# Linear attention and channel mix on one core: the order of work from a table, and q of five batches transposed by the DMA crossbar

## The chip, the core and the metric

The kernel runs on one core of a Trainium2 chip. The core has TensorE (PE, matmuls; its weight loads are shown as PEld), VectorE (DVE), ScalarE (ACT), GpSimd (POOL) and SyncE (SP). Matmuls write to PSUM, which has eight banks per partition; DVE and ACT carry results from PSUM to SBUF. DMAs are issued from the queues of POOL, SP and ACT. Each engine runs its instructions in program order and waits on semaphores.

The metric is the device time of one execution in microseconds, the median of several runs. Times inside the text come from one profiled execution.

## The reference

There are B = 8 batches, H = 8 heads, S = 576 positions, head size 64, so C = 512; the mix has an inner width of 1024.

```python
kv = np.einsum('bhsd,bhse->bhde', k, v)
out = np.einsum('bhsd,bhde->bhse', q, kv)
rms = np.sqrt(np.mean(out * out, axis=-1, keepdims=True) + 1e-06)
x = out / rms * g_norm                       # then heads side by side: (B, S, 512)
x_prev = x moved by one position, zero in front
xk = mu_k * x + (1.0 - mu_k) * x_prev
xr = mu_r * x + (1.0 - mu_r) * x_prev
k = np.maximum(xk @ w_k, 0.0)
v = k * k @ w_v
r = 1.0 / (1.0 + np.exp(-(xr @ w_r)))
return r * v
```

Inputs and output are float32; the kernel computes with bf16 operands, cast on the way in by the loads.

## The kernel before

**Stages.** The work is cut into named pieces, and the names below are those of the table in the change. A number after the name is the batch (attention) or the group (mix), the part after the dot a head pair or a chunk, and `#2` a second piece of the same name.

Attention, per batch, over four head pairs `hp`; everything is held with channels on partitions and positions along the row:
- `loadk`, `loadv`, `loadq` (L314): from DRAM, 96 positions rows by heads, cast to bf16, on POOL's queue. Batch 0 comes in pieces of two heads, batch 1 in halves, the others whole. In batch 0 the first two heads come instead by `first_load` (L264), uncast, on SP's and ACT's queues, and are cast on DVE (L302).
- `kv` (L545): k times v for a head pair, on PE; `kvc`: its two diagonal blocks to SBUF.
- `qtr` (L572): q transposed on PE, 24 transposes of a 96x64 block for two head pairs; `qc` (L580): PSUM to the tile qT.
- `u` (L594): kv times qT on PE; `uc`: to the tile uT. `sq`: its square on DVE. `ss` (L620): sum over the channels of a head by a matmul with ones. `ln`, `exp` (L624, L628): the inverse root on ACT. `mul` (L641): x, into the tile xT, with a short copy that makes the shifted column block. `d`: x minus x_prev. `xk`, `xr` (L667): d scaled by a column (tile md) plus x_prev, into rings `xk`, `xr` of four batches.

Batch 0 has functions of its own (L381 on) that cut it finer, so that the mix can start early.

Mix, per group g of 512 positions, nine groups: `k` (eight chunks, L715), `relu` on ACT, `ksq` on DVE; `r` (four chunks, L766) and `sig` on ACT; `v` (four chunks in two parts); `out` on DVE, the product; `store` on SP (L696). `k`, `r` and `v` pieces are four matmuls of 128x512 each. Group 0's `k` is done in two halves, `k0.a` per head pair and `k0.b`. Group 1 needs the xk of batches 0 and 1.

**Weights.** `w_k0`, `w_k1`, `w_r`, `w_v` come on POOL's queue (L337); the first three are scaled by g_norm on DVE (`g.w_k0` and so on, L342).

**Buffers.** k, v, q, qT, uT and xT have two buffers, out has three. PSUM has two rings of two tiles of two banks: `mm` for the mix, `at` for the attention, batch 0 too.

**Order.** Every piece is added to a planner (L39) with the engines it may run on, the pieces it waits for, the buffers it uses, a duration and a due time. `run` (L78) places the pieces one by one by its own estimates, takes the due times of the STAGES list for the attention and T0 + TG * g for the mix, and then writes the instructions out in that order; each engine's order is fixed by it. While PE has a gap before the last of `k0.a`, `filler` (L684) puts matmuls of a zero tile there, their number from the gap's estimated length. In POOL's order the loads of batch 0 come first, then w_k0, w_k1, w_r, w_v, then batch 1 and the others.

Of the kernel before, what the change touches and what calls it, by code (L numbers as in the profile page):

```python
# [7 lines left out]
FP32 = mybir.dt.float32  # L8
# [4 lines left out]

class Buf:
    def __init__(self, tag):
        self.tag, self.users, self.t, self.placed = tag, [], None, False


class Piece:
    def __init__(self, on, fn, deps, bufs, due, rel, land, mode, table, name):  # L20
        self.on, self.fn, self.due, self.rel, self.land = on, fn, due, rel, land
        self.mode, self.table, self.name = mode, table, name
        self.deps = [d for d in deps if d is not None]
        self.bufs = list(bufs)
        for b in self.bufs:
            b.users.append(self)
        self.eng = self.start = self.end = None
        self.emitted = False


class Planner:
    TAIL = {"PE": 0.17, "ACT": 0.09, "DVE": 0.08, "POOL": 0.1, "SP": 0.0}
    LAT = {"PE": 0.06, "ACT": 0.06, "DVE": 0.06, "POOL": 0.1, "SP": 0.0}
    TO_PE = 0.1
    SWITCH = 0.1
    TABLE = 1.3
    COLD = 8.0
    WAIT = {"PE": 0.04, "ACT": 0.04, "DVE": 0.04, "POOL": 0.04, "SP": 0.04}

    def __init__(self, rings):  # L40
        self.rings = {tag: [None] * n for tag, n in rings.items()}
        self.left = []

    def add(self, on, fn, deps=(), bufs=(), due=0.0, rel=0.0, land=0.0, mode=None, table=None, name=""):
        p = Piece(on, fn, deps, bufs, due, rel, land, mode, table, name)
        self.left.append(p)
        return p

    def backward(self):
        after = {}  # L50
        for p in self.left:
            for d in p.deps:
                after.setdefault(d, []).append(p)

        def due(p):
            if p.due is None:
                us = min(p.on.values()) + max(self.TAIL[e] + self.LAT[e] for e in p.on) + 0.05
                p.due = min((due(s) for s in after.get(p, ())), default=1e6) - us
            return p.due

        for p in self.left:
            due(p)

    def room(self, bufs):
        t, want = 0.0, {}
        for b in bufs:
            if not b.placed:
                want.setdefault(b.tag, set()).add(b)
        for tag, bs in want.items():
            for old in self.rings[tag][:len(bs)]:  # L70
                if old is None:
                    continue
                if any(u.end is None for u in old.users):
                    return None
                t = max([t] + [u.end + 0.1 for u in old.users])
        return t

    def run(self, slack, filler=None, warm=None):  # L78
        self.backward()
        free, order, dma, hw = {}, [], 0.0, 0.0  # L80
        mode, table = "full", "ln"
        while self.left:
            best = {}
            for p in self.left:
                if any(d.end is None for d in p.deps):
                    continue
                room = self.room(p.bufs)
                if room is None:
                    continue
                ways = []  # L90
                for eng, us in p.on.items():
                    t = max(free.get(eng, 0.7), room, p.rel)
                    for d in p.deps:
                        if d.eng == eng and not d.land:
                            t = max(t, d.start + d.us + (0.05 if eng in ("ACT", "DVE") else 0.0))
                            continue
                        lat = self.LAT[d.eng]
                        if eng == "PE":
                            lat += self.TO_PE + slack(p)
                        t = max(t, d.end + lat)  # L100
                    late = 0.0
                    if eng == "PE" and p.mode != mode:
                        us = us + self.SWITCH
                    if eng == "PE" and t < self.COLD:
                        us = us * 1.9
                    if eng == "ACT" and p.table and p.table != table:
                        us, late = us + self.TABLE, 2.5 if p.table == "ln" else 0.0
                    ways.append((t + us, t, eng, us, late))
                _, t, eng, us, late = min(ways)
                best.setdefault(eng, []).append((t, p.due + late, p, us))  # L110
            picks = []
            for eng, c in best.items():
                t0 = min(x[0] for x in c)
                win = self.WAIT[eng]
                picks.append(min((x for x in c if x[0] <= t0 + win), key=lambda x: x[1] + x[0] * 0.1) + (eng,))
            t, _, p, us, p.eng = min(picks, key=lambda x: x[0])
            if p.eng == "PE":
                if filler and warm.end is None:
                    gap = t - free.get("PE", 0.7)
                    fill = filler(gap, free.get("PE", 0.7) > self.COLD)  # L120
                    if fill is not None:
                        n, fn = fill
                        f = Piece({"PE": 0.0}, fn, (), (), 0, 0, 0, "full", None, "idle%d" % n)
                        f.eng, f.start, f.end, f.us = "PE", free.get("PE", 0.7), t, gap
                        order.append(f)
                mode = p.mode
            if p.eng == "ACT" and p.table:
                table = p.table
            p.start, p.us = t, us
            free[p.eng] = t + us  # L130
            p.end = t + us + self.TAIL[p.eng]
            if p.land:
                if p.eng == "POOL":
                    dma = max(dma, t + us + 2.4) + p.land
                    p.end = dma + 1.3
                else:
                    hw = max(hw, t + us + 1.4) + p.land
                    dma = max(dma, hw)
                    p.end = hw + 1.3
            for b in p.bufs:  # L140
                if not b.placed:
                    b.placed = True
                    self.rings[b.tag].append(b)
                    self.rings[b.tag].pop(0)
            self.left.remove(p)
            order.append(p)
        for p in order:
            p.fn(p.eng)
            p.emitted = True
        return order  # L150
# [3 lines left out]
def kernel(  # L154
# [76 lines left out]
    def act_us(n, sbuf=False, ap=False):  # L231
        return 0.1 + n / 1200 + (0.03 if sbuf else 0.0) + (0.09 if ap else 0.0)
# [638 lines left out]
```

## Time and profile before

| | us |
|---|---|
| median of 5 runs (lowest, highest) | 224.34 (223.82, 225.93) |
| the profiled execution, its own time | 223.96 |
| its span, first to last instruction | 222.2 |
| PE busy | 205.1 |
| DVE busy | 154.1 |
| ACT busy | 134.8 |
| POOL busy | 27.3 |

In the span, PE's share is 92%; since matmuls are pipelined and their ends are modelled, idle time says more than that share. The granted clock of PE is 1.0 but for a stretch between 10 and 20 us. The page's slices show the DMA engines busy without a break up to about 72 us and little used afterwards, while PE has its gaps in the first third.

```profile
PE   8698779987998999999999999999999999999991
PEclk9959999999999999999999999999999999999999
DMA  6999999999999379537963300330033024016033
```

Each of 40 slices is 5.6 us; a digit is the busy share in tenths.

### The profile page before, as it was taken

The page shows a single profiled execution, that of the slowest core. Times are in us where ns is not written, and L with a number is a line of the kernel's source. Part 1 is how long each engine was busy: PE and PEld are TensorE (multiplying, and loading weights), DVE is VectorE, ACT ScalarE, POOL GpSimd, SP SyncE. Part 2 cuts the span into 40 slices and gives each one's busy share as a digit, 9 for nine tenths or more (in the row PEclk, how much of TensorE's full clock was granted, in tenths as well). Part 3 has the DMA queues.
Part 4 walks back from the last instruction along what each step waited for, and adds up shares of the span by engine and source line. Part 5 has one row for each costly group of instructions (what it writes and reads, how often), then busy time and mean ns, then how long its engine had stood idle before and what let it go on. Part 6 is the DMA issues. An engine that isn't in the chain of part 4 may idle for free.

```text
span 222.2 us, 4343 instructions
## 1 busy us (share of the span) xinstructions
PE 205.1 (92%) x1756; PEld 113.1 (51%) x1779; DVE 154.1 (69%) x311; ACT 134.8 (61%) x180; POOL 27.3 (12%) x42
## 2 busy tenths in 40 slices
PE   8698779987998999999999999999999999999991
PEld 8456555554554544454445864554444444444450
DVE  3459995699769999799928992999299424224231
ACT  2269364977489957964796479657965705504600
POOL 7862114042100021002100000000000000000000
PEclk9959999999999999999999999999999999999999
DMA  6999999999999379537963300330033024016033
GB/s 171 198 206 206 204 202 205 203 244 225 223 203 178 98 115 216 85 96 93 222 101 97 94 3 0 94 97 1 3 94 96 0 69 123 0 25 165 3 94 94
DMA packets 27592, 26.95 MB, mean 121 GB/s; under 512 B 1836, under 2 KB 23092, under 8 KB 27572
## 3 DMA queue, kind: packets, MB, share of 16 engines
q0 software_dynamic: 21008, 16.34, 47.8%
q1 hardware_dynamic: 5892, 9.45, 15.5%
q10 hardware_dynamic: 672, 0.89, 1.2%
q8 instruction: 14, 0.23, 0.4%
q14 instruction: 6, 0.05, 0.1%
HBM read 33.56 MB, written 9.44 MB: 194 GB/s over the span
## 4 chain that ended last, share of the span: by engine, by line
PE 50%; DMA 21%; DVE 15%; issue 4%; ACT 3%; POOL 3%; SPq 2%; POOLq 0%; DVEq 0%
PE mm L721 16%; PE mm L790 16%; PE mm L769 11%; DMA k<-in_k_dram 8%; DMA q<-in_q_dram 7%; DVE out L794 3%; DMA out_dram<-out 3%; DMA v<-in_v_dram 3%; DVE qT L222 3%; DVE md L669 2%; DVE sqk L728 2%; PE at L807 2%; PE at L596 2%; SPq L704 2%; PE mm L807 2%
## 5 line engine op out<-in xcount | busy, mean ns | idle before, releaser
L725 ACT ACTIVATE relu<-mm 128x1024 bf16<-128x1024 f32 x36 | 36.8, 1023 | 45.9 <-PE mm L721 39.1
L721 PE MATMUL mm<-xk,w_k 128*128 128x512 bf16 (+1 forms) x278 | 59.1, 355 | 1.2 <-issue 0.9
L790 PE MATMUL mm<-w_v,sqk 128*128 128x512 bf16 x248 | 57.6, 379 | 1.3 <-ACT sig L774 0.8
L794 DVE TENSOR_TENSOR out<-mm,sig 128x1024 f32<-128x1024 f32 x16 | 19.6, 1223 | 30.8 <-ACT ln L626 12.9
L790 PEld LDWEIGHTS <-sqk 128*128 128x128 bf16 x256 | 24.9, 98 | 28.2 <-issue 1.3
L721 PEld LDWEIGHTS <-w_k 128*128 128x128 bf16 x288 | 27.0, 98 | 24.1 <-issue 0.3
L769 PE MATMUL mm<-w_r,xr 128*128 128x512 bf16 x140 | 32.9, 380 | 1.6 <-DVE xr L492 1.3
L728 DVE TENSOR_TENSOR sqk<-relu 128x1024 bf16<-128x1024 bf16 x32 | 22.0, 687 | 9.9 <-ACT relu L725 9.8
L774 ACT ACTIVATE sig<-mm 128x1024 bf16<-128x1024 f32 x18 | 18.2, 1023 | 7.5 <-PE mm L769 7.3
L769 PEld LDWEIGHTS <-xr 128*128 128x128 bf16 x144 | 14.0, 98 | 16.9 <-DVE xr L492 1.9
L626 ACT ACTIVATE ln<-at,eps 128x576 f32<-128x576 f32 x28 | 19.3, 741 | 0.6 <-PE at L622 0.3
L229 ACT ACT_TABLE_LOAD x14 | 18.0, 1283 | 1.4 <-PEq L855 1.2
L669 DVE TENSOR_SCALAR md<-d,cols 128x576 bf16<-128x576 bf16 x56 | 18.5, 372 | 0.2
L630 ACT ACTIVATE rs<-ln 128x576 bf16<-128x576 f32 x28 | 17.8, 689 | 0.1
L220 ACT CAST uT<-at 128x576 bf16<-128x576 f32 (+1 forms) x25 | 15.0, 605 | 2.8 <-PE at L596 2.1
L316 POOL DMA_DIRECT2D k<-in_k_dram x11 | 8.0, 729 | 54.3 <-PE at L549 51.1
L220 ACT CAST kvb<-at 64x256 bf16<-64x256 f32 (+2 forms) x14 | 4.4, 316 | 14.3 <-PE at L549 7.8
L596 PE MATMUL at<-qT,kvb 128*128 128x288 bf16 x56 | 11.3, 286 | 1.8 <-ACT qT L220 0.9
L222 DVE COPY qT<-at 128x1152 bf16<-128x1152 bf16 (+2 forms) x17 | 11.1, 655 | 1.9 <-PE at L414 1.2
L692 PE MATMUL mm<-zero 128*128 128x128 bf16 x89 | 10.9, 285 | 1.1 <-DVE zero L271 1.1
L644 DVE TENSOR_TENSOR xT<-uT,rs 128x1152 bf16<-128x1152 bf16 x14 | 10.5, 750 | 1.1 <-ACT rs L630 1.1
L610 DVE TENSOR_TENSOR sq<-uT 128x1152 bf16<-128x1152 bf16 (+1 forms) x16 | 10.7, 678 | 0.6 <-ACT uT L220 0.3
(68 smaller groups left out, 200.3 us busy)
## 6 DMA issues: line engine op xcount, KB each, us to landing
out_dram<-out SPq DMA_DIRECT2D x22, 192.0 KB, 2.5
k<-in_k_dram POOLq DMA_DIRECT2D x6, 576.0 KB, 10.7
v<-in_v_dram POOLq DMA_DIRECT2D x6, 576.0 KB, 13.7
q<-in_q_dram POOLq DMA_DIRECT2D x6, 576.0 KB, 13.9
out_dram<-out SPq DMA_DIRECT2D x23, 128.0 KB, 2.4
out_dram<-out SPq DMA_DIRECT2D x22, 64.0 KB, 2.2
w_k<-in_moe_w_k_dram POOLq DMA_DIRECT2D x2, 512.0 KB, 8.5
w_v<-in_moe_w_v_dram POOLq DMA_DIRECT2D x1, 1024.0 KB, 15.6
```

The costliest lines, as they stand in the source:

```text
L220: nc.scalar.copy(out=dst, in_=src)
L229: nc.scalar.preload_act_table_set(name)
L626: nc.scalar.activation(out=get(ln), in_=ps.t[:, :, 0:HS], func=AF.Ln, bias=eps, scale=1.0 / HD)
L630: nc.scalar.activation(out=get(rs)[:, hp].rearrange("q (i c) -> q i c", i=2), in_=ln.t, func=AF.Exp, scale=-0.5)
L669: nc.vector.tensor_scalar(out=get(md)[:, hp], in0=d.t[:, hp], scalar1=cols[:, m0 + hp:m0 + hp + 1], scalar2=None, op0=ALU.mult)
L721: nc.tensor.matmul(get(ps)[:, fc % 2, a0:a1], w_k_sb[:, cc, 128 * fc:128 * fc + 128], xk[:, cc, x0:x0 + a1 - a0], start=(cc == 0), stop=(c ...
L725: nc.scalar.activation(out=get(rt), in_=ps.t, func=AF.Relu)
L728: nc.vector.tensor_mul(out=get(sqk)[:, 2 * f2:2 * f2 + 2, :], in0=rt.t, in1=rt.t)
L769: nc.tensor.matmul(get(ps)[:, ci % 2, :], xr[:, cc, n0:n0 + 128], w_r_sb[:, cc, :], start=(cc == 0), stop=(cc == NHP - 1))
L774: nc.scalar.activation(out=get(sg), in_=ps.t, func=AF.Sigmoid)
L790: nc.tensor.matmul(get(ps)[:, ci % 2, :], sqk.t[:, fc, 128 * ci:128 * ci + 128], w_v_sb[:, fc, :], start=(fc == 0), stop=(fc == NFC - 1))
L794: nc.vector.tensor_mul(out=get(ot)[:, xs, :], in0=ps.t[:, xs, :], in1=sg.t[:, xs, :])
```

## The change

1. The planner's search is gone. The order of all pieces, with the engine of those that have a choice and the number of idle matmuls in each gap, is a table in the file; `run` writes the pieces out in that order.
2. For batches 3 to 7 (`BY_DMA`) the pieces `qtr` and `qc` are replaced: `ql` copies q of a head pair into a tile `q2` (one buffer) with the two heads of the pair side by side, on DVE or ACT, and `qt` is one DMA per batch on SP's queue that transposes q2 into qT.
3. Batch 0 uses a PSUM ring of four single-bank tiles (`a1`). When the first tile of a later batch is asked for, that pool is released and the two-bank ring `at` is made in its place.
4. In batch 0 the scaling of d by a column is a piece of its own per head pair (`mk`, `mr`), on DVE or ACT, and `k0.a` may add up its head pairs in any order.
5. The first loads of v and q in batch 0 go with the others on POOL; k's stays on SP and is cast by ACT.
6. The shifted column block of `mul` is made by a second product instead of a copy.
7. From batch 4 on, the pieces that write the xk and xr rings also wait for the k and r pieces that read what they overwrite.

The table, cut after the last q transfer:

```diff
+ORDER = """
+loadq0.4 loadv0.6 loadk0.6 loadq0.6 setup loadv0.4 ident idle:42 kv0.3 qtr0.2 table loadk0.4 loadk0.2 qtr0.3
+qc0.3:DVE qc0.2#2:ACT idle:5 kv0.2 qc0.2:DVE kvc0.3#2:ACT small qc0.3#2:ACT kvc0.3:DVE idle:2 u0.3 kvc0.2#2:ACT
+kvc0.2:ACT idle:4 u0.2 first_k uc0.3:DVE sq0.3 u0.2#2 uc0.2#2:ACT loadq0.2 loadq0.0 idle:14 qtr0.0 cast_k:ACT qtr0.1
+uc0.2:DVE qc0.0#2:DVE ident9 qc0.1#2:ACT loadv0.2 qc0.0:DVE kv0.1 kvc0.1:ACT kvc0.1#2:ACT ss0.3 ln0.3 exp0.3
+qc0.1:DVE idle:7 u0.1 sq0.2 idle:1 ss0.2 uc0.1:DVE loadv0.0 sq0.1 ln0.2 tr9 cols exp0.2 kv0.0 kvc0.0:ACT idle:8
+ss0.1 sq0.2#2 kvc0.0#2:DVE idle:8 u0.0#2 ln0.1 u0.0 exp0.1 edge mul0.2 uc0.0#2:ACT uc0.0:DVE sq0.0 mul0.3 sq0.0#2
+loadv1.4 d0.2 mr0.2:DVE loadk1.4 ss0.2#2 ln0.2#2 exp0.2#2 idle:18 ss0.0 mul0.2#2 d0.2#2 ln0.0 exp0.0 loadv1.0 idle:7
+ss0.0#2 ln0.0#2 exp0.0#2 idle:25 kv1.2 kvc1.2:ACT mul0.1 d0.3 loadq1.0 qtr1.0 mul0.0 mk0.3:DVE d0.1 mul0.0#2
+mk0.1:DVE d0.0#2 kvc1.2#2:ACT d0.0 loadk1.0 idle:5 kv1.0 qc1.0:ACT loadq1.4 mr0.1#2:DVE kvc1.0#2:ACT mr0.3#2:ACT
+mr0.2#2:DVE idle:19 qtr1.2 kvc1.0:DVE u1.0 w_k1 xk0.3 qc1.2:DVE idle:13 u1.3 mr0.0:ACT uc1.0:ACT mk0.0:ACT uc1.3:ACT
+mk0.2:DVE xk0.2 u1.1 xk0.1 xk0.0 g.w_k1 mk0.2#2:DVE mk0.1#2:DVE xr0.0 mk0.0#2:ACT uc1.1:ACT w_k0 sq1.0 sq1.1 xk0.0#2
+idle:22 k0.a1.2 g.w_k0 mr0.3:ACT u1.2 mr0.0#2:ACT k0.a1.0 k0.a1.3 mk0.3#2:DVE xr0.2#2 ss1.0 uc1.2:ACT ln1.0 k0.a1.1
+w_r xk0.2#2 ss1.1 relu0.01 k0.a0.0 exp1.0 sq1.2 g.w_r:DVE k0.a0.3 k0.a0.1 sq1.3 xr0.2 k0.a0.2 relu0.00 ksq0.00
+ksq0.01 mr0.1:ACT k0.b1 xr0.1 k0.b0 ln1.1 w_v xr0.0#2 relu0.11 xr0.3 ksq0.11 ss1.2 relu0.10 ksq0.10 loadq2.0 exp1.1
+mul1.0 ss1.3 ln1.2 loadk2.0 r0.0 r0.1 sig0.0 v0.0.0 v0.0.1 v0.1.0 v0.1.1 out0.0 d1.0 xk1.0 exp1.2 ln1.3 exp1.3
+mul1.2 qtr2.2 d1.2 qc2.2:ACT r0.2 r0.3 sig0.1 xk1.2 v0.2.0 v0.2.1 v0.3.0 loadv2.0 kv2.0 kvc2.0#2:DVE loadq3.0
+kvc2.0:ACT ql3.2:ACT qtr2.0 ql3.3:DVE ql3.1:ACT v0.3.1 out0.1 ql3.0:DVE xr1.0 qc2.0:DVE k1.0 loadv3.0 k1.1 relu1.0
+u2.2 uc2.2:DVE qt3 k1.2 k1.3 relu1.1 ksq1.0 k1.4 k1.5 u2.3 uc2.3:ACT u2.0 uc2.0:DVE loadk3.0 k1.6 xr1.2 u2.1
+uc2.1:DVE loadq4.0 ql4.0:DVE relu1.2 k1.7 kv3.0 ksq1.2 relu1.3 r1.0 kvc3.0#2:ACT r1.1 sq2.0 ql4.1:DVE kvc3.0:ACT
+u3.1 ql4.2:DVE u3.0 r1.2 r1.3 store0.1 ql4.3:DVE ksq1.1 uc3.1:ACT uc3.0:ACT sig1.0 u3.3 ss2.0 ksq1.3 loadv5.0
+store0.0 v1.0.0 sig1.1 v1.0.1 loadv4.0 uc3.3:DVE ln2.0 ss2.1 ln2.1 sq2.2 exp2.0 v1.1.0 v1.1.1 out1.0 exp2.1 mul2.0
+loadk4.0 u3.2 store0.0#2 uc3.2:ACT ss2.2 loadk5.0 v1.2.0 ln2.2 exp2.2 ss2.3 sq3.0 sq3.2 v1.2.1 ln2.3 exp2.3 d2.0
+kv4.0 kvc4.0:ACT loadq5.0 kvc4.0#2:ACT kv5.0 store0.1#2 mul2.2 kvc5.0:ACT xk2.0 ss3.2 kvc5.0#2:ACT ln3.2 exp3.2 d2.2
+v1.3.0 ss3.3 ln3.3 xk2.2 ss3.0 ln3.0 exp3.3 qt4 v1.3.1 out1.1 xr2.0 ss3.1 u4.0 ln3.1 exp3.1 k2.0 k2.1 uc4.0:ACT
+xr2.2 relu2.0 exp3.0 u4.1 uc4.1:ACT k2.2 ksq2.0 k2.3 relu2.1 sq4.0 mul3.2 k2.4 d3.2 u4.3 uc4.3:ACT mul3.0 d3.0 u4.2
+uc4.2:ACT xk3.2 k2.5 loadv6.0 k2.6 k2.7 store1.0#2 relu2.2 ksq2.2 xk3.0 r2.0 r2.1 ksq2.1 relu2.3 ksq2.3 ql5.2:ACT
+xr3.2 ss4.1 loadk6.0 loadq6.0 r2.2 r2.3 sig2.0 sig2.1 ln4.1 exp4.1 ss4.0 k3.0 k3.1 ln4.0 relu3.0 store1.0 loadk7.0
+v2.0.0 ql5.1:DVE v2.0.1 v2.1.0 v2.1.1 ql5.0:DVE sq4.2 ss4.2 ln4.2 ss4.3 exp4.0 ql5.3:DVE v2.2.0 v2.2.1 qt5 out2.0
+ln4.3 v2.3.0 xr3.0 v2.3.1 ql6.3:ACT ksq3.0 exp4.3 exp4.2 out2.1 mul4.2 d4.2 ql6.0:DVE k3.2 k3.3 u5.2 uc5.2:DVE
+ql6.1:ACT relu3.1 ksq3.1 k3.4 k3.5 u5.0 relu3.2 ksq3.2 mul4.0 k3.6 k3.7 uc5.0:ACT relu3.3 u5.3 ksq3.3 u5.1 r3.0 r3.1
+uc5.1:DVE store1.1#2 uc5.3:ACT sq5.2 sq5.0 sig3.0 store2.0 store2.0#2 d4.0 xk4.0 kv6.0 kvc6.0#2:DVE r3.2 r3.3
+ql6.2:ACT ss5.1 sig3.1 kvc6.0:ACT store1.1 v3.0.0 v3.0.1 v3.1.0 ss5.3 store2.1 ln5.3 ln5.1 v3.2.0 store2.1#2 v3.1.1
+v3.2.1 loadv7.0 v3.3.0 xk4.2 out3.0 ss5.0 xr4.2 v3.3.1 out3.1 qt6 exp5.3 exp5.1 ss5.2 ln5.2 ln5.0 k4.0 k4.1 relu4.0
+k4.2 k4.3 relu4.1 u6.2 ksq4.0 xr4.0 u6.3 store3.0#2 loadq7.0 uc6.3:DVE exp5.0 exp5.2 uc6.2:DVE sq6.2 k4.4 k4.5
+relu4.2 k4.6 k4.7 mul5.0 u6.0 uc6.0:DVE ksq4.1 ksq4.2 relu4.3 mul5.2 ss6.3 ln6.3 ksq4.3 r4.0 r4.1 u6.1 sig4.0 kv7.0
+uc6.1:ACT r4.2 d5.2 xk5.2 d5.0 kvc7.0#2:ACT kvc7.0:DVE r4.3 xk5.0 sig4.1 sq6.0 v4.0.0 v4.0.1 ql7.2:ACT v4.1.0
+store3.0 v4.1.1 ql7.3:ACT store3.1 ql7.0:ACT v4.2.0 v4.2.1 ss6.2 v4.3.0 ql7.1:DVE v4.3.1 out4.0 store4.0 ln6.2 k5.0
+exp6.2 store3.1#2 out4.1 exp6.3 xr5.2 k5.1 relu5.0 ss6.1 k5.2 k5.3 ksq5.0 ln6.1 xr5.0 mul6.2 d6.2 k5.4 k5.5 relu5.1
+k5.6 exp6.1 k5.7 ss6.0 ksq5.1 xr6.2 relu5.2 relu5.3 ksq5.3 ln6.0 ksq5.2 r5.0 r5.1 qt7 u7.2 uc7.2:DVE store4.1 u7.3
 ...
```

The parts that make it work:

```diff
-    def run(self, slack, filler=None, warm=None):
...
+    def run(self, filler):
+        for token in ORDER:
+            name, _, eng = token.partition(":")
+            if name == "idle":
+                filler(int(eng))
+                continue
+            p = self.pieces[name]
+            assert not p.emitted and all(d.emitted for d in p.deps), name
+            p.fn(eng or p.on[0])
             p.emitted = True
...
+        "a1": (4, (128, 512), FP32),
+        "q2": (1, (NP, NHP, NJ, 2 * HD), BF16),
...
+            if buf.tag == "at" and len(at_pool) == 1:
+                at_pool[0].release()
+                at_pool[0] = pool = tc.alloc_tile_pool(name="psum_at", bufs=2, space=bass.MemoryType.PSUM,
+                                                       reuse_waits="tile")
...
+        if b in BY_DMA:
+            q2 = Buf("q2")
+            parts = []
+            for hp in range(NHP):
+                def q_relay(eng, hp=hp):
+                    copy(eng, get(q2)[:, hp].rearrange("p j (e d) -> p e j d", e=2),
+                         qin.t[:, 2 * hp:2 * hp + 2, :].rearrange("p e (j d) -> p e j d", j=NJ))
...
+            def q_turn(_):
+                nc.sync.dma_start_transpose(out=get(qT).rearrange("q i (j p) -> q (i j) p", j=NJ),
+                                            in_=q2.t.rearrange("p i j c -> p (i j c)"))
...
-        for hp0, n in groups[2]:
+        for hp0, n in groups[2] if b not in BY_DMA else ():
...
-                nc.vector.tensor_copy(out=xT.t[:, hs, 1:NP], in_=xT.t[:, hs, S:S + NP - 1])
+                nc.vector.tensor_mul(out=xT.t[:, hs, 1:NP], in0=uT.t[:, hs, S - NP:S - 1], in1=rs.t[:, hs, S - NP:S - 1])
```

A token such as `qc0.3:DVE` names a piece and its engine, `idle:42` is 42 idle matmuls. Pieces without an engine have one alone: PE for `kv`, `qtr`, `u`, `ss`, `k`, `r`, `v`; DVE for `sq`, `mul`, `d`, `xk`, `xr`, `ksq`, `out`; ACT for `ln`, `exp`, `relu`, `sig`; POOL for loads and weights; SP for `qt` and `store`.

## The prediction

> **What bounds the kernel now.** I read the windows by stage first, then the chain of waits, then the groups by form. The windows were cut where TensorE (PE) passes from one kind of work to the next; columns are length, busy us (instructions) per engine, granted clock, DMA share, GB/s.
>
> ```profile
> 0.00:17.90 17.90, 14.66 (x175) 11.07 (x175) 9.16 (x35) 7.64 (x18) 12.85 (x23) 0.81 1.09 193
> 17.90:26.58 8.68, 6.72 (x64) 4.97 (x64) 8.41 (x32) 6.01 (x11) 1.45 (x2) 1.00 1.26 206
> 38.05:54.75 16.70, 14.03 (x222) 8.43 (x223) 14.36 (x27) 13.72 (x23) 4.60 (x6) 1.00 1.29 221
> 68.31:182.02 113.71, 111.62 (x903) 58.90 (x917) 90.71 (x165) 80.74 (x103) 4.61 (x6) 1.00 0.43 85
> ```
>
> From 68.31 on PE is busy 98% of the time, DVE 80%, ACT 71%: every us of PE work taken out there shortens the run, if nothing else becomes late. Before that the DMA runs without a pause at about 204 GB/s, and PE waits. The chain of waits names for whom:
>
> ```profile
> 13.46 18.45 DMA k<-in_k_dram
> 38.17 15.68 DMA q<-in_q_dram
> 53.89 0.70 PE at L577 x24
> 54.75 3.40 PE mm L721 x15
> 123.67 0.63 PE at L577 x24
> 217.46 0.61 PE at L807 x4
> ```
>
> It passes through batch 1's k (landed at 31.91), then batch 3's q (landed at 53.85): its transposes stand in PE's order ahead of k1 (group 1's first product), which starts at 54.75. The last row ends PE's work at 218.07. The groups by form give the prices:
>
> ```profile
> L577 PE MATMUL at<-ident,q 96*64 96x96 bf16 x336 | 9.8, 208 | 0.6 <-DMA q<-in_q_dram 0.6
> L222 DVE COPY qT<-at 128x1152 bf16<-128x1152 bf16 x13 | 9.8, 755 | 0.6 <-PE at L577 0.5
> L222 DVE CAST k<-out 96x768 bf16<-96x768 f32 x1 | 0.6, 556 | 1.1 <-DMA out<-in_k_dram 1.1
> L645 DVE COPY xT<-xT 128x190 bf16<-128x190 bf16 x14 | 3.2, 225 | 0.5
> ```
>
> **Part 1, the transposes leave PE.** The chain shows 24 transposes (half a batch) taking 0.63 us back to back. Ten halves go, 6.3 us. Before has one of them (batch 3's first) ahead of k1, nine after it: 9 x 0.63 = 5.7 us off the stretch that PE fills.
>
> What comes in: 20 relay copies of 96x768 bf16, 11 on DVE and 9 on ACT by the table. No row shows one. On DVE it lies between 0.225 (190 columns) and 0.556 us (same shape from f32); I take 0.45, as the shape is the latter's: 5.0 us, against ten qT copies of 0.755 = 7.6 us that go. On ACT it lies between 0.64 (576-column cast) and 1.12 us (1152-column copy); I take 0.80: 7.2 us. The table also moves five 576-column uT copies of batches 1 to 7 from ACT (0.64 each) to DVE (0.75), and one qT copy of batches 1 and 2 the other way. Net: DVE 5.0 - 7.6 + 3.8 - 0.8 = +0.4 us on 154, ACT 7.2 - 3.2 + 1.1 = +5.1 on 135. Beside PE's 98% this is covered; if that cover were gone, these 5 us would be the price.
>
> **Part 2, the crossbar transfer.** One per batch, 576 KB, on SP's queue. Nothing in the trace is one, so its time L from the last relay to the landing has bounds only. From below: a 192 KB store lands in 2.5 us and a 64 KB one in 2.2; continued by that slope 576 KB take 3.4, with 0.5 of issue 3.9. Inside the loading stage the same stores took 5.0 to 6.6. From above: a 576 KB cast load waited 15.7 us, queued. I take 5, nearest to the stores, since it too is a hardware queue's transfer. It cannot cost below nothing beyond part 1, since it runs on no engine.
>
> The relay buffer is single and four waits hang on it. DVE's first relay of batch 4 waits for transfer 3, with ksq1.2 (a square of group 1's relu) and all later DVE work behind it; the first relays of batch 5 wait for transfer 4; ACT's of batch 6 for transfer 5, with relu3.1, for which PE's PSUM tile waits, behind; ACT's of batch 7 for transfer 6. And PE waits with u (q times kv) of each batch. The cover is the work that the table puts between a batch's last relay and the waiting piece, at 0.865 us per piece of k, r or v. Batch 3: 10.5 us on PE, but 6.4 on DVE (two xr at 1.33, four copies at 0.75, a ksq at 0.69) before its relay of batch 4. Batch 4: 11. Batch 5: six pieces, 5.2. Batch 6: 11. Batch 7: 8 (9.1 and a piece, less an output product and two stores that SP has before it). At L = 5 all are covered, batch 5 by 0.2 us. On SP a late transfer also holds the output stores behind it; the out ring is three deep, and SP waited 21 us for DVE at the longest, so that is free.
>
> Here a row and two rules meet. The row: a batch's 48 transposes take 1.26 us of PE. The Trainium skill's "VectorE: DVE Perf Modes", in Rules for kernel authors, says to transpose on TensorE where a PSUM destination will do, and prices a crossbar 128x128 at 1309 ns (The three transpose paths); 24 such tiles in series would be an estimate of 31 us, and batch 5 alone would stall 26. Its "DMA: Bandwidth & Descriptors" (Latency and other measured facts) gives 261 GB/s, an estimate of 2.3 us for 576 KB. No row of this case decides between them.
>
> **Part 3, the head.** Batch 1's loads move ahead of the four weight loads on POOL; v's and q's first loads leave ACT's and SP's queues for POOL (two more issues of 0.64 us). The first product needs POOL's third load, issued at 2.67; the second landed 5.93 us after its issue, so it starts near 8.6, not at 6.08. In before, w_v landed at 10.49 + 15.6 = 26.1 us after 4288 KB (batch 0's 1728, weights 2560); the next 1152 KB landed by 31.91, so 199 KB/us. After, w_k1 is complete at 3456 + 512 = 3968 KB: 24.5 us; w_k0 27.1, w_r 29.6, w_v 34.8, batch 2 43.5, q of batch 3 46.4.
>
> So k0 begins late: w_k1 at 24.5 plus its scaling 0.75 = 25.3, against 17.9. But then PE has work in a row: k0 7.0, batch 1's rest 1.2, r0's half 1.7: to 35.2, when w_v is there (by 0.4 us); v0 6.9, q transposes of batch 2 1.3, r0's rest 1.7, kv2 0.9: k1 can start at 46.0. Batch 2's k and v land at 43.5, and kv2's turn, three pieces before k1, is at 43.6. DVE's rows up to xk1.2, which k1 needs, sum to 33 us from 8.6 on: 41.6, which leaves it 4.4 us of waits. With so little to spare in both I add 2.5 us and take 48.5 for k1.
>
> The batch-0 edits (four single-bank tiles in place of two two-bank ones, seven of sixteen md scalings on ACT, accumulation in any order, 111 more idle matmuls in PE's waits) have no price of their own: they decide how much of those 4.4 us is used. The single-bank tiles are given back before batch 1's first two-bank tile (kv1) is written, so kv1 waits for batch 0's last ln: ACT's rows up to there sum to 10.2 us from 8.6 on, 18.8 with no wait, and kv1's data land at 16.1. Nothing but idle matmuls and kv1's own followers stands behind it on PE; in before kv1 ran at 29.94, so this is free. The second xT product in place of the 225 ns copy is nothing: the same columns on the same engine. The added waits of batches 4 to 7 on readers of the xk ring are long past. Stores and tail keep their form.
>
> **The sum.** Before, k1 to PE's end is 218.07 - 54.75 = 163.3. Take off 5.7; add what the table moves behind k1 (u of batch 2, kv of batch 3, one ss piece: 1.0 + 0.9 + 0.2 = 2.1): 159.7. PE ends at 48.5 + 159.7 = 208.2, 9.9 earlier. The profiled run was 223.96 (span 222.2, 1.76 around it), the median 224.34, so it serves as it is: 223.96 - 9.9 = 214.
>
> **Rivals.**
> (A) The head gains nothing: DVE's and ACT's queues, which stand nearly full in the rows 17.90 to 54.75, hold k1 at 54. Then PE ends at 213.7, 4.4 earlier: 219.6. For it: DVE busy 8.41 of 8.68 there. Against: batch 1's data come 13 us sooner (21.9 for 34.8), and DVE idled 4.4 of the 15 us from 30 to 45, waiting for them.
> (B) Slower: the transfer takes L = 13 or more. Place: u of each batch, through qT, and DVE through the single relay buffer. Stalls beyond the covers above: 6.6 (DVE, batch 4's relay) + 2 + 7.8 + 2 + 5 = 23.4 us: 237. It decides from L = 10 on, where 3.6 + 0 + 4.8 + 0 + 2 = 10.4 eats the gain. For it: nothing in the trace moves 2-byte elements apart. Against: every hardware-queue row is at 6.6 or under.
> (C) The table's timing is off on the chip: queues in a fixed order wait for each other in the denser stretch from 48 to 90, at 1 us for each of six groups, and batch 5's cover is short by 2: 222, no change.
> (D) Better than forecast: k1 at 46.0, and half of the 3.6 us that PE stood idle between k1 and its end in before gone: 214 - 2.5 - 1.8 = 209.7.
>
> **How the numbers follow.** My forecast, with covers holding and k1 between 46 and 51, 0.62 together with (D): 209.5 to 217. (A) 0.18. (C) 0.10. (B) 0.10. A measurement here tells 1% from no change, 2.2 us. Below 222.1 lie the forecast, (A) and a little of (C): 0.82. Within 1%: 0.08. Above: 0.10. The range 209.5 to 220.5 takes in (A), and leaves out (B) and most of (C).
>
> **What would show it.** k1's first product (128x512 on xk) at 48.5 and not 54; qT's transfers landing within 5 us; no TensorE idle ended by a DMA into qT after 60 us, the likeliest place for one being batch 5; TensorE's share of busy time after k1 at 97% or more; no qT copy on DVE for batches 3 to 7. Wrong would be: rows of u waiting for qT, ACT or DVE idle until the crossbar's landing, or k0's first product after 29 us.

## The result, and the profile after

| | before | after |
|---|---|---|
| median of all runs (lowest, highest), us | 225.73 (223.82, 227.68) | 227.40 (226.41, 229.62) |
| ratio, 95% interval | | 1.009 (1.0073 to 1.0107) |
| the profiled execution, us | 223.96 | 226.87 |
| its span, us | 222.2 | 225.1 |
| first k1 product, end of PE's work, us | 54.75, 218.07 | 48.55, 221.1 |

The change makes the kernel 0.9% slower; 214.0 was forecast, a gain of 4.6%. PE reaches group 1 six microseconds sooner, as forecast, and ends three later. The slices of the page after the change, 5.6 us each, against those of before:

```profile
PE   8699999999588489999499999999999999999971
PEclk9999999999999679999999999999999999999999
DMA  5999999999999999919915410094014006024033
```

PE's gaps of the first third are gone (busy with idle matmuls and early work), but there is a new hole in the 11th to 15th slice, 56 to 84 us, and a 4 at 107, where PE was nearly full before. In the hole the granted clock falls to 0.6 and 0.7. The DMA engines are at 9 through all of it. Windows cut at k1 (48.31), after the hole, and where the attention is done; columns are length, busy us (instructions) of PE, PEld, DVE, ACT, POOL, granted clock, DMA share, GB/s:

```profile
48.31:85.00 36.69, 27.96 (x262) 14.98 (x264) 23.96 (x45) 23.73 (x36) 8.15 (x11) 0.91 1.27 212
85.00:183.80 98.80, 94.64 (x576) 49.19 (x585) 80.60 (x152) 72.38 (x88) 0.77 (x1) 1.00 0.47 96
183.80:221.10 37.30, 35.10 (x167) 16.39 (x168) 11.66 (x17) 12.29 (x12) 0.00 (x0) 1.00 0.27 74
```

PE is idle for 8.7 us of the first 36.7, for 4.2 of the next 98.8 and for 2.2 of the tail. Together 172.8 us from k1 to the end, 157.7 of it busy. Before it was 163.3 and 159.7:

```profile
54.75:218.07 163.32, 159.70 (x1155) 81.94 (x1172) 112.68 (x196) 101.92 (x125) 5.38 (x7) 1.00 0.47 94
```

The forecast took 5.7 off the busy time, added 2.1, and left the 3.6 of idle time as they were: 159.7. The 13.1 us that are missing are thus 11.5 of new idle time and 1.6 more of busy time than was reckoned, which goes with the slower clock below.

What ended PE's idle time from k1 on, in us, times, and the longest:

```profile
PE at L580 <- DMA qT<-q: 5.9, 3, 3.3
PE at L514 <- DMA k<-in_k_dram: 4.3, 2, 3.2
PE mm L793 <- DVE out L800: 1.4, 1, 1.4
PE mm L702 <- ACT relu L706: 1.3, 1, 1.3
...
```

L580 is `u`, waiting for the crossbar; L514 is `kv`, waiting for k of batches 4 and 5; L793 is the last group's v; L702 is `k`, waiting for a PSUM buffer that a late relu still holds. The transfers themselves, with the time of the issuing instruction (min, median, max in ns), then who waited for them, then their landing:

```profile
L546 SPq DMA_TRANSPOSE qT<-q x5: 2987/3008/7691, 50.6 to 147.2; - x5
...
  ACT q L182: 5.1, 1
  DVE q L184: 5.1, 1
...
DMA to landing us min/median/max: 11.9/15.2/18.6
```

The landing row knows two of the five: batch 3's, issued at 50.60 and landed at 62.45 (11.9), and batch 4's, 65.04 to 83.62 (18.6). For the others it is read from who waits, from the last packet and from the semaphore that tells of the landing: batch 5 from 99.52 to 108.7 (9.2), batch 6 from 119.0 to 124.4 (5.4, its last packet; the last of sixteen updates of its semaphore comes at 125.4, and nobody waits for it), batch 7 from 147.2 to 152.3 (5.1, its semaphore). Batch 5's has a load of batch 6 beside it. SP's queue in the hole, start and length:

```profile
50.60 7.13 SPq L546 DMA_TRANSPOSE qT<-q  x1
...
65.04 7.69 SPq L546 DMA_TRANSPOSE qT<-q  x1
```

The issue alone holds SP for 7 to 8 us for batches 3 and 4, in the loading stage, and for 3 later on. And PE there, with the idle time before each row in brackets:

```profile
62.59 0.65 PE L580 MATMUL at<-qT,kvb 128*128 128x288 bf16 x4 [3.27 <-DMA qT<-q]
72.80 0.95 PE L514 MATMUL at<-v,k 96*64 96x64 bf16 x48 [1.07 <-DMA k<-in_k_dram]
76.98 1.49 PE L514 MATMUL at<-v,k 96*64 96x64 bf16 x48 [3.23 <-DMA k<-in_k_dram]
83.67 0.42 PE L580 MATMUL at<-qT,kvb 128*128 128x288 bf16 x2 [0.84 <-DMA qT<-q]
```

The 48 products of kv5 take 1.49 us where those of kv4 took 0.95: this is the slow clock, 0.50 in this stretch:

```profile
75.00:80.00 5.00, 2.80 (x52) 2.09 (x54) 2.81 (x5) 1.45 (x3) 2.58 (x4) 0.50 1.28 191
```

### The profile page after: what moved, and what is told of

The parts are those of the page before. It is cut to its first block, busy times and chain, and to the rows that moved or that the text cites. A ratio compares the mean times of both kernels' runs of the same rounds, so it can differ in the third digit from the quotient of the medians.

```text
span 225.1 us, 4093 instructions
## 1 busy us (share of the span) xinstructions
PE 202.5 (90%) x1631; PEld 115.7 (51%) x1650; DVE 147.8 (66%) x306; ACT 142.5 (63%) x193; POOL 28.4 (13%) x44
## 5 line engine op out<-in xcount | busy, mean ns | idle before, releaser
L702 PE MATMUL mm<-xk,w_k 128*128 128x512 bf16 (+1 forms) x283 | 57.8, 355 | 1.8 <-ACT relu L706 1.3
L706 ACT ACTIVATE relu<-mm 128x1024 bf16<-128x1024 f32 x36 | 36.7, 1023 | 30.1 <-PE mm L702 28.3
L702 PEld LDWEIGHTS <-w_k 128*128 128x128 bf16 x288 | 28.2, 98 | 27.1 <-issue 2.1
L776 PEld LDWEIGHTS <-sqk 128*128 128x128 bf16 x256 | 25.3, 99 | 28.4 <-issue 0.9
L780 DVE TENSOR_TENSOR out<-mm,sig 128x1024 f32<-128x1024 f32 x16 | 19.6, 1222 | 23.8 <-PE mm L776 10.8
L610 ACT ACTIVATE ln<-at,eps 128x576 f32<-128x576 f32 x28 | 20.1, 737 | 7.1 <-PE at L606 6.9
L672 PE MATMUL mm<-zero 128*128 128x128 bf16 x200 | 17.2, 250 | 1.1 <-DVE zero L231 1.1
L672 PEld LDWEIGHTS <-zero 128*128 128x128 bf16 x200 | 15.1, 114 | 1.9 <-DVE zero L231 1.1
L580 PE MATMUL at<-qT,kvb 128*128 128x288 bf16 x56 | 10.2, 286 | 5.9 <-DMA qT<-q 5.9
L628 DVE TENSOR_TENSOR xT<-uT,rs 128x1152 bf16<-128x1152 bf16 x14 | 10.5, 751 | 7.3 <-ACT rs L614 7.3
L264 POOL DMA_DIRECT2D q<-in_q_dram x12 | 8.6, 717 | 42.6 <-PE at L561 21.0
L182 ACT CAST uT<-at 128x576 bf16<-128x576 f32 x15 | 9.3, 635 | 6.2 <-PE at L580 6.1
L606 PE MATMUL at<-sq,ones 128*128 128x288 bf16 x56 | 11.4, 302 | 0.0
L264 POOL DMA_DIRECT2D v<-in_v_dram x12 | 8.5, 708 | 22.2 <-PE at L514 21.4
## 6 DMA issues: line engine op xcount, KB each, us to landing
w_v<-in_moe_w_v_dram POOLq DMA_DIRECT2D x1, 1024.0 KB, 18.6
```

Of the source, the lines that this page charges most:

```text
L610: nc.scalar.activation(out=get(ln), in_=ps.t[:, :, 0:HS], func=AF.Ln, bias=eps, scale=1.0 / HD)
L672: nc.tensor.matmul(get(k_ps[1])[:, 0, 0:128], zero[:, 0:128], zero[:, 128:256], start=not k_seen[1], stop=not k_seen[1])
L702: nc.tensor.matmul(get(ps)[:, fc % 2, a0:a1], w_k_sb[:, cc, 128 * fc:128 * fc + 128], xk[:, cc, x0:x0 + a1 - a0], start=(cc == 0), stop=(c ...
L706: nc.scalar.activation(out=get(rt), in_=ps.t, func=AF.Relu)
L776: nc.tensor.matmul(get(ps)[:, ci % 2, :], sqk.t[:, fc, 128 * ci:128 * ci + 128], w_v_sb[:, fc, :], start=(fc == 0), stop=(fc == NFC - 1))
L780: nc.vector.tensor_mul(out=get(ot)[:, xs, :], in0=ps.t[:, xs, :], in1=sg.t[:, xs, :])
```

## The experiments

The theory, T: the order in the table reckons with transfers that are much shorter than they are; every loss but the tail's comes from transfers that land late and from pieces that stand ahead of their data. The rival: the table's order as such is at fault, and the transfer does no harm. Where a time was taken in several rounds its ratio to the kernel before on the same chip is given; the others are single executions, read by their profile.

**No crossbar, same table.** In the table the pieces `ql` and `qt` of all five batches go, and `qtr` and `qc` are put between the others where the table has room for them; two places are shown.

```diff
-    BY_DMA, FINE = (3, 4, 5, 6, 7), {}
+    BY_DMA, FINE = (), {}
...
-k1.5 u2.3
+k1.5 qtr3.0 qc3.0:DVE u2.3
...
-uc3.3:DVE ln2.0
+uc3.3:DVE qtr4.0 qc4.0:DVE ln2.0
...
```

> The changed kernel with q of batches 3 to 7 transposed on TensorE again (two transposes' pieces and two DVE copies per batch in place of four relay copies and one crossbar transfer); the rest of the table as it is. Theory T (the crossbar transfer is what lost the gain): k1 starts at 48.5 as in the changed kernel, the waits of TensorE for qT (5.9 us) and the half-clock stretch around 75 to 82 us are gone, the first v product of group 2 comes some 10 us earlier than in the changed kernel; with 5.7 us of transposes back in TensorE's stretch the time is about 220 (217.5 to 222). Rival C (the table is out of step by itself, for instance kv4 and kv5 placed before their loads): TensorE still idles 8 us or more between 57 and 85 and the time stays above 225.

Measured: 224.39 us, ratio 0.996 (0.992 to 0.999). This is between what the two expected. PE's longest waits after k1:

```profile
PE mm L791 <- DVE out L798: 1.4, 1, 1.4
PE at L604 <- ACT uT L180: 0.7, 1, 0.7
```

No wait is over 0.8 us but the tail's 1.44, and the clock is 1.0 from k1 to PE's end. So the hole comes with the transfers, yet the table brings almost nothing without it: k1 comes 5.3 us sooner (first weights at 49.2 for 54.5), and from there to the last weights it is 169.2 us for 163.2. Of the 6.0 us, 2.1 are the pieces that the table moved behind k1, 1.6 the tail (9.2 us from the first v8 weights to the last, 7.6 before), and the rest is many waits under 0.8.

**Crossbar for batches 5, 6 and 7 only.** In the table, batches 3 and 4 as in the version above.

```diff
-    BY_DMA, FINE = (3, 4, 5, 6, 7), {}
+    BY_DMA, FINE = (5, 6, 7), {}
```

> Only batches 5, 6 and 7 use the crossbar; batches 3 and 4, whose transfers run while the loads still fill the DMA engines, are transposed on TensorE. Theory T with contention (transfers and loads take from each other): no idle of TensorE above 1 us between 57 and 95, the loads of batch 4's and 5's k land 4 us sooner than in the changed kernel (by 68.5 and 72.5 instead of 72.8 and 77.0), batch 5's stall at its first u (1.8 us) and the one behind ACT's late exps (1.3 us) stay: about 218 (216 to 220.5). Without contention as a cause, only 3.3 + 0.8 us come back and the time is 223.

Measured: 223.35 us, ratio 0.989 (0.984 to 0.994). The longest of PE's waits:

```profile
PE at L578 <- DMA qT<-q: 2.2, 1, 2.2
PE mm L791 <- DVE out L798: 1.4, 1, 1.4
PE mm L700 <- ACT relu L704: 1.3, 1, 1.3
```

This is the time that was expected without contention (223), not T's 218. Beside the version above, six halves less on PE (3.8 us) bring 1.0, since 3.5 come back: batch 5's u waits for its transfer, and ACT's first relay of batch 6 stands 5.5 us before the same transfer has read the single buffer, with a relu behind it. (The 0.7 between the two sums is less than the spread of the first version's runs, 223.57 to 225.96.) The waits for k of batches 4 and 5 are gone as well, and the reason is in the loads: here T's contention shows, though not in the time. Their rows (landing in us) in the windows of 57 to 64 us, first the changed kernel, then this one:

```profile
k<-in_k_dram POOLq DMA_DIRECT2D x2, 576.0 KB, 15.9
```

```profile
k<-in_k_dram POOLq DMA_DIRECT2D x2, 576.0 KB, 9.4
```

The transfers do not only wait for the loads, they hold the loads back: k of batch 5 lands at 76.94 with them and at 71.86 without, though it is issued 2.1 us later there (72.76 and 68.95 for batch 4's).

**Plain moves in the place of the transfers.**

```diff
-                nc.sync.dma_start_transpose(out=get(qT).rearrange("q i (j p) -> q (i j) p", j=NJ),
-                                            in_=q2.t.rearrange("p i j c -> p (i j c)"))
+                flat = q2.t.rearrange("p i j c -> p (i j c)")
+                qf = get(qT).rearrange("q i s -> q (i s)")
+                nc.sync.dma_start(out=qf[0:NP, :], in_=flat[:, 0:NHP * S])
+                nc.sync.dma_start(out=qf[NP:128, :], in_=flat[0:128 - NP, 0:NHP * S])
```

> The crossbar transfer is replaced by two plain moves of the same 576 KB from the relay tile into qT on the same queue; q of batches 3 to 7 is not transposed, so this part of the computation is left out. Theory T' (the transposing makes the transfer slow): the moves land within 3 to 7 us, TensorE does not wait for qT by more than 1 us in all, time 213 to 217. Rival (any move of that size takes this long in this place): landing after 9 us or more and a time within 2 us of the changed kernel.

Measured: 221.4 us, above the 213 to 217 that T' expected and well below the rival's. The output of this version is not the reference's. One move takes 432 KB, the other 144. Issue and landing of the moves, and PE's wait that stays:

```profile
L547 SPq DMA_DIRECT2D qT<-q x5: 552/556/622, 51.3 to 141.8; - x5
L548 SPq DMA_DIRECT2D qT<-q x5: 582/595/596, 52.0 to 142.4; - x5
...
DMA to landing us min/median/max: 3.8/4.1/7.4
```

```profile
PE at L513 <- DMA k<-in_k_dram: 6.2, 2, 3.1
```

The same bytes at the same place of the table, not transposed, land in 7.0 to 7.4 us among the loads and in about 4 later, each move by itself; from the first issue to the last landing it is 7.6 us for batch 3 and 4.4 for batches 5 and 6, against 11.9 to 18.6 among the loads and 5 to 9 later. No u waits. The forecast's 5 us fits the transfer with idle DMA engines alone. The waits for k remain and are longer, because PE arrives sooner and k lands at 72.1 and 76.1, less than 1 us earlier than under the crossbar: it is mostly the bytes that hold the loads, not the transposing.

**One transfer per head pair**, 144 KB each, in the place of one per batch; each u waits for its own.

```diff
-                nc.sync.dma_start_transpose(out=get(qT).rearrange("q i (j p) -> q (i j) p", j=NJ),
-                                            in_=q2.t.rearrange("p i j c -> p (i j c)"))
+                nc.sync.dma_start_transpose(out=get(qT)[:, hp].rearrange("q (j p) -> q j p", j=NJ),
+                                            in_=q2.t[:, hp].rearrange("p j c -> p (j c)"))
```

> One transfer per head pair (144 KB) instead of one per batch, issued one after the other at the same place; each u waits for its own. If the transfer's length goes with the amount (3.0 us of issue and about 8 to 9 us to landing for 576 KB outside the loading stage): a quarter takes 0.75 us of issue and the first lands within 4 us, batch 5's first u no longer waits, about 223. If each transfer has a large fixed part: the four of a batch land one after another at 5 us or more each, batch 5's stalls grow, above 230.

Measured: 229.52 us, between the two sums and nearer to the second. Waits of PE:

```profile
PE at L514 <- DMA k<-in_k_dram: 5.2, 2, 3.0
PE mm L703 <- ACT relu L707: 4.5, 1, 4.5
```

The waits for qT fall from 5.9 to 1.4 us, but four issues take 1.2 us each on a quiet queue, 4.9 for 3.0, so the last one lands later, and ACT's relay of the next batch waits for that one, the buffer being single. The loss moved from u to the relay.

**The transfer alone, with the planner of before.** The pieces `ql` and `qt` are those of the change, with the due times of `qtr` and `qc` and a landing of 3.0.

```diff
+    BY_DMA = (3, 4, 5, 6, 7)
+        "q2": (1, (NP, NHP, NJ, 2 * HD), BF16),
...
+        if b in BY_DMA:
+            q2 = Buf("q2")
...
-        for hp0, n in groups[2]:
+        for hp0, n in groups[2] if b not in BY_DMA else ():
```

> The kernel before with one part of the change alone: q of batches 3 to 7 copied into a buffer and turned by the crossbar, with the order left to the planner of before (it reckons with a landing after some 6 us). Theory T (a transfer takes 9 us or more wherever the loads still run, and 5 to 8 after, against the 5 us that was reckoned with): u of the batches 3 to 5 waits for it, 3 to 8 us in all, while ten half-batches times 0.63 us leave TensorE: 224 to 231 us, not below before's 225.8 by more than 1%. Rival R (the transfers do no harm of themselves, it is the fixed order that has the rest of the work in the wrong place): the 5.7 us less of TensorE come out of the time, about 220 us, and no idle time of TensorE of over 1 us is ended by a transfer.

Measured: 228.33 us. PE's wait, and the landings:

```profile
PE at L617 <- DMA qT<-q: 12.2, 2, 11.2
```

```profile
DMA to landing us min/median/max: 5.2/8.6/17.8
```

Batch 3's transfer, issued at 56.26 with the loads running, lands 17.8 us later and costs 11.2 of PE; the later ones land after 4.9 to 9.7 and cost 1.0 in all. R falls: in an order that does not come from the table the transfer does the same harm.

**The tail.**

```diff
-v8.0.0 v8.0.1 v8.1.0 v8.1.1 out8.0#2 store8.0#2 sig8.1 v8.2.0 v8.2.1 out8.0 store8.0
+v8.0.0 v8.0.1 sig8.1 out8.0 store8.0 v8.1.0 v8.1.1 out8.0#2 store8.0#2 v8.2.0 v8.2.1
```

> The changed kernel with three entries of the table moved: in group 8 the sigmoid of the second pair and the product and stores of the first 128 rows stand directly behind the first v product, as in the order of before. Theory T (ScalarE's share of the stores stands ahead of that sigmoid, and the product of the first rows behind that of the second, so that TensorE waits 1.44 us for a PSUM buffer): the 1.44 us wait near 216.7 goes, the first to the last weights of the last v step take 7.6 us as before, not 9.2, and the run ends 1.4 to 1.6 us earlier than after's 227.4: 225.8 to 226.0. Rival: the end is set by the last stores' landing, and the time stays within 0.5 us of 227.4.

Measured: 225.14 us. All waits of PE from 200 us on:

```profile
PE at L792 <- DVE out L799: 0.5, 1, 0.5
```

The 1.44 us wait is gone, and first to last weights of v8 are 7.6 us again. The span is 1.7 shorter than that of after. The time is 0.7 below what T expected; in this one execution the waits of the hole differ too (for qT 4.4 us and for k 2.8, where after has 5.9 and 4.3), so the rows of the tail are the evidence and not the total. In the table a store, part of which ACT issues, stood ahead of ACT's last sigmoid, and a product that was ready stood behind one that was not.

**kv of batches 4 and 5 later.**

```diff
-kv4.0 kvc4.0:ACT loadq5.0 kvc4.0#2:ACT kv5.0 store0.1#2 mul2.2 kvc5.0:ACT xk2.0 ss3.2 kvc5.0#2:ACT
+loadq5.0 store0.1#2 mul2.2 xk2.0 ss3.2
...
-v1.3.1 out1.1
+v1.3.1 kv4.0 kvc4.0:ACT kvc4.0#2:ACT out1.1
...
-k2.4 d3.2
+k2.4 kv5.0 kvc5.0:ACT kvc5.0#2:ACT d3.2
```

> The changed kernel with the kv products of batches 4 and 5 and their copies moved back in the table, behind the last product of v1 and into k2. Theory T (the two stood ahead of their loads, which land at 72.8 and 77.0): the waits of 1.07 and 3.23 us go, with them the half clock from 75 to 80, and the first u of batch 4 is reached earlier; but the transfer of batch 4 lands at 83.6 in the profile of after, so part of it turns into a longer wait there: k2 then starts no later than after's 83.8, and the time lies between 221 us (the transfer is faster beside less work) and 227 us (it lands as late as ever). Rival R1 (the landing of the transfer of batch 4 alone sets this stage): 227 to 228 us, the wait for qT of batch 4 grows from 0.84 to over 4 us.

Measured: 227.1 us.

```profile
PE at L579 <- DMA qT<-q: 5.4, 2, 3.2
```

The waits for k are gone, and PE waits 3.18 us at 81.51 for the transfer of batch 4 instead; the slow clock, 0.50, is now at 80 to 85. This is R1's time; the wait is shorter than its 4 us, as the transfer lands 2.2 us earlier than in after, at 81.37. In this stage the transfer's landing was next, and a repair of the other wait alone brings nothing.

**Cover for the transfers**: the version with crossbar for 5, 6 and 7, in which batch 5 is copied and sent earlier, with two buffers and the tail repaired.

```diff
-        "q2": (1, (NP, NHP, NJ, 2 * HD), BF16),
+        "q2": (2, (NP, NHP, NJ, 2 * HD), BF16),
...
-k2.5 loadv6.0 k2.6 k2.7 store1.0#2 relu2.2 ksq2.2 xk3.0 r2.0 r2.1
+ql5.1:DVE k2.5 loadv6.0 k2.6 ql5.0:DVE k2.7 store1.0#2 relu2.2 ql5.2:ACT ksq2.2 xk3.0 ql5.3:DVE r2.0 qt5 r2.1
```

> The version with q of 3 and 4 transposed on TensorE and the crossbar for 5, 6 and 7 (223.35 us), with the copies and the transfer of batch 5 placed some 8 us earlier, two buffers for the copied q, and group 8 in before's order. Theory T (a transfer costs TensorE nothing where it has 10 us and no copy stands waiting for it): the waits of 2.19 us (qT of batch 5), 1.34 us (relu behind a copy) and 1.44 us (group 8) go: 223.35 - 2.2 - 1.3 - 1.5 = 218.3 us, 217.5 to 220. Rival R2 (what was waited for is late next at another place, the table having no slack): 221 to 223.5 us. Rival R3 (a transfer placed earlier meets the loads of batches 6 and 7 and takes 12 us or more): the wait for qT of batch 5 remains over 1 us.

Measured: 219.69 us, ratio 0.978 (0.970 to 0.986). This is in T's range, at its upper end. No engine waits for a transfer any more:

```profile
L545 SPq DMA_TRANSPOSE qT<-q x3: 2926/2938/3044, 92.2 to 141.3; - x3
...
DMA to landing us min/median/max: 5.0/7.4/9.8
```

The landing row knows two of the three, batch 6's (5.0) and batch 5's (9.8). Batch 5's is hidden, not shorter. A new wait of 1.45 us stands at 104.6, ended by a product of DVE.

**A store ahead of the transfer.** That product fills an output buffer whose last store stood behind the transfer on SP.

```diff
-k2.7 store1.0#2 relu2.2
+k2.7 store1.0#2 store1.0 relu2.2
...
 ksq2.2 xk3.0 ql5.3:DVE r2.0 qt5 r2.1
...
-relu3.0 store1.0 loadk7.0
+relu3.0 loadk7.0
```

> The version of 219.69 us with one store of group 1 moved ahead of the transfer of batch 5 on SyncE's queue. Theory T (that store, issued behind the transfer, lands so late that the product of group 2 waits for its buffer and TensorE 1.45 us for that product): the 1.45 us near 104.6 goes: 218.2 us, 217.6 to 219. Rival: the product is held by something else, and the wait stays: 219.5 us or more.

Measured: 217.77 us, ratio 0.962 (0.956 to 0.969): the fastest here that computes the reference's result, faster than before and after. The product on DVE, first in the version above, then in this one:

```profile
103.29 1.22 DVE L779 TENSOR_TENSOR out<-mm,sig 128x1024 f32<-128x1024 f32 x1 [2.82 <-PE at L579]
```

```profile
100.81 1.23 DVE L779 TENSOR_TENSOR out<-mm,sig 128x1024 f32<-128x1024 f32 x1 [0.71 <-PE mm L775]
```

The first names u on PE as the releaser, which the product does not need; that the store was the cause is shown by moving it. PE's wait is gone.

**No crossbar, tail repaired.** The first version with the tail's order of before.

> The version with all five batches transposed on TensorE (224.39 us) with group 8 in before's order: what the fixed order gives with no crossbar at all. Theory T (the tail's 1.5 us is independent of the rest): 222.5 to 223.2 us; the version with the crossbar for 5, 6 and 7 under cover is then 3 to 4.5 us below it, six halves times 0.63 us being 3.8. Rival: the tail is covered by something here and the time stays at 224 or more.

Measured: 222.76 us, ratio 0.985 (0.979 to 0.992). The crossbar for 5, 6 and 7 is worth 5.0 us beside it once it is covered: 3.8 for six halves, the rest not told apart.

**The table with transfers that cost little**: plain moves, kv of 4 and 5 later, tail repaired.

> The changed kernel with plain moves of the same bytes in the place of the crossbar transfers (q of batches 3 to 7 is left untransposed, so the output is not the reference's), and with two other repairs: the kv products of batches 4 and 5 stand later, and group 8 is in before's order. Theory T (beside the length of the transfer, all that the forecast missed is the two waits for k of batches 4 and 5 with the slow clock after them, and the tail): the plain moves alone gave 221.4; 6.2 us of waits, about 0.5 us of slow clock and 1.5 us of the tail go: 213 to 215 us, which is the forecast's 214.0. Rival R (the table has no slack and each repaired wait comes back at another place, as the later kv products did under the crossbar): 217 us or more.

Measured: 214.57 us, one execution, of a version whose output is not the reference's. PE from its first k1 weights to its end:

```profile
49.20:208.80 159.60, 156.47 (x1018) 79.44 (x1016) 116.34 (x211) 108.47 (x135) 8.99 (x12) 1.00 0.58 124
```

159.6 us, 156.5 of them busy: the forecast's stretch (159.7 and 156.1) to a few tenths. The rival, that each repaired wait comes back elsewhere, falls where the transfer, the two waits for k and the tail are repaired together.

## Why the prediction was wrong, point by point

**What bounds the kernel: right.** PE is the bound from k1 on: its busy share there fell from 98% to 91% and the time rose with its waits. With them repaired the time follows PE's work, in the last experiment to a few tenths.

**Part 1, transposes off PE and relays: right.** The relays took 0.35 us on DVE (0.45 taken) and 0.83 on ACT (0.80), within the bounds:

```profile
L184 DVE COPY q<-q x11: 345/349/597, 48.4 to 143.4; 96x768 bf16<-96x768 bf16 x11
L182 ACT COPY q<-q x9: 815/830/832, 48.7 to 142.2; 96x768 bf16<-96x768 bf16 x9
```

They are hidden beside PE's work but where a relay stands on a buffer that a transfer still reads.

**Part 2, the transfer's length L = 5: this is the step that failed.** L was taken "nearest to the stores, since it too is a hardware queue's transfer". Measured from the issue: 11.9, 18.6, 9.2, 5.4 and 5.1 us. So 5 is about right for a transfer with idle DMA engines (4.9 to 5.4 us over all versions with whole transfers), and wrong for batches 3, 4 and 5: one length was taken for five places. Two things were missed. First, the bound from above, 15.7 us of a queued load, was the nearer row for batches 3 and 4: they are sent while the DMA engines have no pause. There the transfer is also far dearer than a plain move of its bytes, 11.9 us for 7.6 in batch 3's place, where with idle engines it is 4.9 to 5.4 for 4.4. Second, the forecast reckoned the loads up to q of batch 3 into one stream at 199 KB/us, but gave the 1152 KB of two transfers, and the loads of batches 4 and 5 that run beside them, no place in it; the two transfers are worth 5.8 us of that stream by themselves.

Of the covers one came out and the others did not. DVE's first relay of batch 4 was reached 6.9 us after the issue (6.4 reckoned). PE reached u of batch 3 after 8.7 us (10.5), of batch 4 after 17.8 (11; the waits for k and the slow clock lie in between) and of batch 5 after 7.4 (5.2). ACT's first relay of batch 6, which waits for batch 5's transfer, was named among the waits but got no cover of its own: it was reached 4.1 us after the issue, too early for an L of 5 too. So the stalls are L less cover: 3.3, 0.8 and 1.8 us on PE, and 5.1 on ACT's relay of batch 6 with 1.3 of PE behind it. The stores behind a transfer on SP, put at nothing there ("so that is free"), were free only as long as other waits were longer: with those repaired one of them cost 1.45 us.

Of the two rules weighed there, the estimates of 31 us by the Trainium skill's "VectorE: DVE Perf Modes" (The three transpose paths) and of 2.3 by its "DMA: Bandwidth & Descriptors" (Latency and other measured facts), neither gave the time: an undisturbed transfer took 4.9 to 5.4. The first page's advice (Rules for kernel authors), to transpose on TensorE, held for batches 3 and 4 (223.35 us for 227.40) and not for 5 to 7 once their transfers are covered (222.76 for 217.77).

**Part 3, the head: right, by its margin.** k1's first product was at 48.55 us (48.5 forecast). The rows had summed to 46.0, and 2.5 were added by judgement; k0's first product came at 27.70 and not at 25.3, and from there to k1 it was 20.9 us for 20.7 reckoned. That the margin was the size of the delay is luck.

**The sum: two terms were not in it.** The waits for k of batches 4 and 5, 4.3 us with some 1.6 of slow clock after them, and the tail's 1.5. "Stores and tail keep their form" overlooked that the table reverses two products and puts ACT's store ahead of its last sigmoid; both stood in the table. The waits for k are the other side of Part 2: they are gone where no transfer runs among the loads. One piece stays without a name: the same table without any crossbar loses some 2 us in many short waits (first experiment), which the last one, at 3.1 us of idle time in all, does not show.

**The rivals.** (B) named the mechanism and its places, u through qT and DVE through the single buffer; its point, L from 10 on, was passed for batches 3 and 4 only, so that its price of 237 was too high. It was given 0.10. (C), the fixed order waiting for itself, is right for the tail and for the early kv, and wrong as the main cause, as the transfer alone on the old planner and the last experiment show. (A) and (D) are out.

What stays open is why a transfer suffers so much more among the loads (11.9 us for 4.9 to 5.4) than a plain move (7.6 for 4.4). The two kinds differ in more than the transposing: the trace has the transfer as 2304 packets of 256 bytes and the moves as packets of 4608, and a plain move in small packets was not run. A crossbar transfer of batch 3 or 4 in an order that gives it 20 us of cover was not tried.

## What to carry to other kernels

A transfer put in the place of engine work has to be entered into the sum of the stage's DMA, with its bytes before and behind those of the loads: where the DMA engines have no pause it took two to four times its undisturbed time here, and two of them delayed k of batches 4 and 5 by 4 and 5 us, where their bytes are worth 5.8. Give it the work that is due after the loads are through, a second buffer for what feeds it, and look at what its queue holds behind it. When several waits end within a few microseconds of each other, repairing one may show nothing, as with kv of batches 4 and 5: repair them together before the order is blamed.

## What the runs showed of the hardware

- The same DMA transpose of 576 KB landed 4.9 to 5.4 us after its issue with idle DMA engines, 7.4 in one place beside a load (batch 4 on the planner of before), 9 to 10 in batch 5's place and 10.8 to 18.7 in the loading stage (in batch 6's place of the changed kernel and of two versions the last of sixteen semaphore updates came 6.4 to 6.5 us after the issue, fifteen of them within 4.9); its issue held SP 2.9 to 3.3 us in all cases but the last and 6.4 to 8.0 in the last. Plain moves of the same bytes took 1.1 to 1.2 us of issue everywhere.
- After PE had idled 1.07 and 3.23 us within 5.3, the granted clock was 0.50 from 75 to 80 us and PE's rows there took 1.6 times as long. The length of one wait does not tell whether the clock falls: after the 3.27 us that end at 62.6 it stayed at 1.0, while in the version with kv later a wait of 2.19 us at the same u was followed by a lower clock in the stretch from 60 to 65:

```profile
60.00:65.00 5.00, 2.81 (x11) 1.25 (x11) 2.74 (x7) 2.11 (x3) 1.65 (x3) 0.80 1.23 249
```

- With 11.2 us of idle time (planner of before, transfer alone) the clock was 0.80, 0.50 and 0.67 in the three stretches of 5 us from 65 on.
- A store issued on SP behind a transpose held its output buffer long enough to cost PE 1.45 us; moved ahead of it, nothing.
